# Thresholded attention and a quick-GELU network: scores of the third and fourth pair computed twice, more row sums through DRAM, new ranks

## The chip, the cores and the metric

The kernel runs on one core of a Trainium2 chip. The core has TensorE (matrix products, writing to PSUM), VectorE (DVE in the profile), ScalarE (ACT), GpSimd (POOL) and SyncE (SP, which here only issues DMAs). Each engine executes its own list of instructions strictly in the order in which the program wrote it, and waits on semaphores for the others. The metric is the device time in microseconds of one execution; the times shown are of three runs, and the verdict compares medians.

## The reference

Inputs are q, k, v of shape (8, 8, 576, 64) (batch, heads, sequence, head dimension), a scalar tau, and two float64 weight matrices, 512 x 2048 and 2048 x 512. Cut to what matters:

```python
scores = scale * np.matmul(q, k.transpose(0, 1, 3, 2))
thresh = np.max(scores, axis=-1, keepdims=True) - tau
scores = np.where(scores >= thresh, scores, -1000000000.0)
attn = np.exp(scores - np.max(scores, axis=-1, keepdims=True))
attn = attn / (np.sum(attn, axis=-1, keepdims=True) + 1e-09)
x = np.matmul(attn, v)            # -> (8 * 576, 512), heads side by side
h = x @ w_in
out = (h * (1.0 / (1.0 + np.exp(-1.702 * h)))) @ w_out
```

So each row of scores keeps only what lies within tau of its maximum, and then goes through a softmax. The output of the attention, 4608 tokens of 512, goes through a two-layer network.

## The kernel before

**Pairs.** Two heads of one batch make a pair; there are 32 pairs, n = 0 to 31, four to a batch. Scores stand transposed: keys on the partitions, queries along the free dimension, in nine tiles of 64 keys (j), two of which share an SBUF tile of 128 x 1152 (t = 0 to 3, and a tail of 128 x 576). The steps of a pair are

1. `load_qk`, `load_v`: DMAs from SP; `prep` (L477) transposes q and k on VectorE.
2. `scores` (L493): four 64-row matmuls of 288 columns for each j into PSUM; `keep` (L510) copies the tile to SBUF on ScalarE.
3. `in_groups` with max (L516), `over_tiles` (L525), `over_halves` (L536, L542 or L547): the maximum of each query less tau, on VectorE.
4. These thresholds have to lie along the free dimension on all partitions (the buffer `mb`). For the pairs in `BY_DMA` a small transpose (L553) is followed by two DMAs to a row in DRAM (`row_out`, L566) and two back, spread over the partitions (`row_in`, L575). Pair 2 is not in `BY_DMA`; it uses `spread_max` (L557), a transpose on VectorE.
5. `sub` (L580) subtracts the thresholds on VectorE, `mask` (L586, a steep Prelu) and `exps` (L590) follow on ScalarE.
6. `values` and `sums_by_pe` (both L601, tiles pv and den): products with v, and for pairs 0 to 4 with a matrix of ones. Pairs 5 to 31 sum with `in_groups` (add) on VectorE instead. For pairs 5 to 7 the sums are then spread with `one_group` (L643, L647) and `spread_sums` (L684, L686) on VectorE, from pair 8 on with `turn_sums` (L658 to L663) and DMAs through DRAM (`sums_out`, L668, `sums_in`, L675).
7. `place_x` (L703): divides and writes x, transposed. When the four pairs of a batch are placed, token blocks of 256 can enter the network.

**Weights.** They arrive as float64 in 32 pieces (16 of w_in, then 16 of w_out), by DMAs from POOL (L428, L429), and are turned into float32 by `cv_ex` (L439), `cv_power` (L447, ScalarE), `cv_frac` (L453, L457) and `cv_end` (L465).

**Network.** `mm1_0` (L758), `tanh` and `gelu_0` (L764), `mm2` (L740) do the first two blocks; later blocks use L718, L727, L730 and L909, the last four L823. From pair 7 on the scores of pair n are interleaved with the values of pair n - 2; these stretches are called joints below.

**Order.** The program writes a list of tasks with an engine, an estimated cost, a rank and resources that they take and give back (PSUM slots `psA`, three of them, and `psM`, two; SBUF slots; slots of the DRAM rows). `run_in_order` goes through estimated time and starts on each engine the ready task of lowest rank. Only the order that comes of this is in the program: on the chip, an instruction that waits holds up everything behind it on its engine. The rank of a pair's task is n plus a bias by function, from one table for pairs 0 to 3 (`EARLY`), one for 4 to 7 (`SECOND`) and one for the rest (`LATER`). The weights' tasks have ranks of their own (`W_RANK`, `CV`). Network tasks on TensorE come last in rank and fill what is left, those on the other engines come first.

Of the kernel before, what the change touches and what calls it, by code (L numbers as in the profile page):

```python
# [10 lines left out]
FP32 = mybir.dt.float32  # L11
# [19 lines left out]
def kernel(  # L31
# [84 lines left out]
    stop = const.tile([P, 1], FP32, name="stop")  # L116
    shift = const.tile([P, 1], FP32, name="shift")
# [9 lines left out]
    for x in ("raw0", "raw1", "qkT0", "qkT1", "mb"):  # L127
# [6 lines left out]
        "exps": -11.47,  # L134
        "in_groups": 5.75,
        "keep": 10.66,
        "load_qk": -0.27,
        "load_v": 4.86,
        "mask": -2.66,
        "one_group": -15.86,  # L140
        "one_row": 12.67,
        "over_halves": -7.01,
        "over_tiles": -4.01,
        "place_x": -17.11,
        "prep": -11.73,
        "row_in": 20.49,
        "row_out": 4.47,
        "scores_run": 12.45,
        "spread_max": -1.73,
        "spread_sums": 7.14,  # L150
        "sub": 9.27,
        "sums_by_pe": 0.27,
        "sums_in": -9.39,
        "sums_out": 2.13,
        "turn_rows": -12.55,
        "turn_sums": -0.41,
        "values": 14.64,
        "w_sum": 4.11,
        "x_sum": -14.1,
    }  # L160
    SECOND = {
        "exps": -7.29,
        "in_groups": 20.95,
        "keep": 16.67,
        "load_qk": -8.88,
        "load_v": 5.53,
        "mask": 2.36,
        "one_group": 2.55,
        "one_row": -2.71,
        "over_halves": -12.07,  # L170
        "over_tiles": 2.86,
        "place_x": -20.26,
        "prep": 3.49,
        "row_in": -19.42,
        "row_out": -24.08,
        "scores_run": -7.99,
        "spread_max": -3.11,
        "spread_sums": -2.29,
        "sub": 14.98,
        "sums_by_pe": 35.93,  # L180
        "sums_in": 7.43,
        "sums_out": 4.05,
        "turn_rows": -3.84,
        "turn_sums": 4.03,
        "values": 11.79,
        "w_sum": -10.45,
        "x_sum": -10.98,
    }
    LATER = {
        "exps": 2.01,  # L190
        "in_groups": 10.37,
        "keep": -0.02,
        "load_qk": -6.6,
        "load_v": 3.77,
        "mask": 14.79,
        "one_group": 4.78,
        "one_row": -14.98,
        "over_halves": 1.09,
        "over_tiles": -6.27,
        "place_x": -0.34,  # L200
        "prep": 2.34,
        "row_in": 4.02,
        "row_out": 2.64,
        "scores_run": -11.25,
        "spread_max": -9.44,
        "spread_sums": -6.73,
        "sub": 2.14,
        "sums_by_pe": 1.46,
        "sums_in": 3.78,
        "sums_out": 2.16,  # L210
        "turn_rows": 12.26,
        "turn_sums": 0.29,
        "values": -10.38,
        "w_sum": 6.61,
        "x_sum": 6.02,
    }
    CV = {
        "cv_end": -8.05,
        "cv_ex": 2.22,
        "cv_frac": -11.72,  # L220
        "cv_power": -4.72,
        "load_w": -7.79,
# [4 lines left out]
    QUARTERS = ("scores", "scores_run", "values", "sums_by_pe")  # L227
# [76 lines left out]
    JOINT = 7  # L304

# [183 lines left out]
    def scores(n, j):  # L489
        ps = psA.tile([P, 2, 512], FP32, name="ps", tag="ps")  # L490
        for h in range(2):
            for c in range(2):
                nc.tensor.matmul(  # L493
                    ps[ts(c, KT), h, 0:SH],
                    lhsT=mats[n, 1][ts(h, D), ts(j, KT)], rhs=mats[n, 0][ts(h, D), ts(c, SH)],
                    start=True, stop=True,
                )
        if j == NK - 1:
            del mats[n, 0], mats[n, 1]
        pss[n, j] = ps  # L500
# [31 lines left out]
    def over_halves(n):  # L532
        r = stats[n, ALU.max]
        o = work.tile([P, QB], FP32, name="fold", tag="fold", bufs=1)
        for x in (1, 3) if n in BY_DMA else range(4):
# [3 lines left out]
            )  # L539
        if n in BY_DMA:  # L540
# [10 lines left out]
    def turn_rows(n):  # L551

        nc.vector.transpose(out=flat[1], in_=flat[0])  # L553

# [52 lines left out]
    def values(n, tiles):  # L607
# [4 lines left out]
        if n < NPAIR:  # L612
# [334 lines left out]
    nc.gpsimd.memset(ones, 1.0)  # L947
    nc.gpsimd.dma_start(
# [26 lines left out]
    BY_PE = 5  # L975
    BY_DMA = (0, 1, *range(3, NP))
    SUMS_BY_DMA = range(8, NP)
# [6 lines left out]
    W_RANK = (0, 12.87, 12.51, 22.24, 0, 4.97)  # L984
# [211 lines left out]
    for n in range(NP):  # L1196
# [5 lines left out]
        slow = 1.1 if n < NPAIR else 1.0  # L1202
# [59 lines left out]
        else:  # L1262
            for js in [range(x, x + 3) for x in range(0, NK, 3)] if n >= WHOLE else [[x] for x in range(NK)]:
# [4 lines left out]
                    give=own(n, "qkT0", "qkT1") if js[-1] == NK - 1 else (),  # L1268
# [4 lines left out]
        a = task("DVE", 0.35, r, over_tiles, n, ALU.max, after=mx)  # L1273
        a = task(
            "DVE", 0.8 if n in BY_DMA else 1.05, r, over_halves, n, after=[a, tau_done],
            take=("row",) if n in BY_DMA else (),
        )
        if n in BY_DMA:
            a = task("DVE", 0.21, r, turn_rows, n, after=[a])
            a = task("SP", 0.6, r, row_out, n, after=[a], lag=3.3)  # L1280
# [8 lines left out]
        for t in range(NKT + 1):  # L1289
            tail = t == NKT  # L1290
            a = task(
# [9 lines left out]
        if n < NPAIR:  # L1301

            pv = den = None
            for t in every:
                first = t == 0
                den = task(
                    "PE", (0.97 if t < NKT else 0.484) * slow, r, sums_by_pe, n, [t], True, after=[ws[t], den],
                    take=("psM", "psM") if first else (),
                )
                pv = task(  # L1310
                    "PE", (0.97 if t < NKT else 0.484) * slow, r, values, n, [t], after=[ws[t], den, pv, lv],
                    take=("psA",) if first else (), give=(back[t],) if t < NKT else ("s_t", v_m),
                )
            su = []
            a = task("DVE", 1.07, r, one_row, n, after=[den], give=("psM", "psM"))
        else:
# [3 lines left out]
            if n < BY_PE:  # L1320
                a = task("PE", 4.36, r, sums_by_pe, n, every, False, after=ws + [pv], take=("psA",), give=back)
                a = task("DVE", 1.07, r, one_row, n, after=[a], give=("psA",))
            else:
                su = [
# [51 lines left out]
```

## Time and profile before

| | us |
|---|---|
| median of three runs (lowest, highest) | 1317.49 (1315.77, 1319.47) |
| the profiled execution's own time | 1317.94 |
| its span, first to last instruction | 1316.2 |
| TensorE busy in the span | 1260.9 |
| VectorE busy | 1006.1 |
| ScalarE busy | 646.6 |
| first matmul of the network (L758) starts at | 117.60 |
| last attention write of pair 3 (L703) starts at | 114.40 |

Spans count from the first instruction to the last. Where a table says "idle before" with an arrow, the engine stood still for so long and the arrow names what ended that. Durations of instructions that follow one another directly overlap a little, so a sum over a run of them is made from start to start.

### The profile page before, as it was taken

What the parts mean: (1) busy time and instruction counts of PE and PEld (TensorE: products, weight loads), DVE (VectorE), ACT (ScalarE), POOL (GpSimd) and SP (SyncE); (2) the same over time, 40 slices, a digit from 0 to 9 for tenths busy, and PEclk for the clock granted to TensorE, in tenths of its full rate; (3) what the DMA queues carried; (4) which work ended last, traced back from release to release, by engine and by line L of the source; (5) the groups of instructions that cost most, each with busy time, mean ns of one, the idle gap of its engine ahead of it and who ended that gap; (6) DMA issues with size and microseconds to landing.
All of it is one profiled execution on the core that took longest, in us unless ns stands there. A gap on an engine that the chain in (4) does not pass through costs nothing. (4 is left out here: it accounts for less than half of the span.)

```text
span 1316.2 us, 22807 instructions
## 1 busy us (share of the span) xinstructions
PE 1260.9 (96%) x9128; PEld 975.6 (74%) x9128; DVE 1006.1 (76%) x1610; ACT 646.6 (49%) x830; POOL 249.0 (19%) x291
## 2 busy tenths in 40 slices
PE   5669999999999999999999999999999999999998
PEld 2346864457887777777778888777777778888887
DVE  7989999898888887788777877777888863652642
ACT  4876666576554555555554555454556540210210
POOL 1201211012031211213021303030212117120120
PEclk8879999999999999999999999999999999999999
DMA  8976766545323223212213222323122110000000
GB/s 152 293 189 207 230 207 149 112 77 100 85 55 71 55 55 71 51 50 54 58 42 72 55 71 55 71 55 71 36 55 54 36 46 8 9 1 25 8 0 32
DMA packets 258819, 102.88 MB, mean 78 GB/s; under 512 B 233754, under 2 KB 243994, under 8 KB 258714
## 3 DMA queue, kind: packets, MB, share of 16 engines
q1 hardware_dynamic: 244986, 63.40, 22.4%
q0 software_dynamic: 11360, 37.74, 9.3%
q8 instruction: 71, 1.16, 0.4%
q10 hardware_dynamic: 2368, 0.30, 0.2%
q14 instruction: 34, 0.28, 0.1%
HBM read 87.51 MB, written 9.69 MB: 74 GB/s over the span
## 5 line engine op out<-in xcount | busy, mean ns | idle before, releaser
L516 DVE TRANSPOSE_TENSOR_REDUCE part<-arena 128x36 f32<-128x1152 f32 (+1 forms) x295 | 357.5, 1235 | 41.9 <-ACT arena L510 32.4
L718 PE MATMUL hps<-xT,w_in 128*128 128x256 f32 x1536 | 337.2, 380 | 0.5 <-DVE arena L730 0.4
L718 PEld LDWEIGHTS hps<-xT,w_in 128*128 128x128 f32 x1536 | 290.7, 190 | 45.9 <-issue 5.7
L586 ACT ACTIVATE arena<-arena 128x1152 f32<-128x1152 f32 (+1 forms) x160 | 169.4, 1059 | 144.0 <-DVE arena L580 143.8
L510 ACT COPY arena<-ps 128x576 f32<-128x576 f32 x288 | 170.7, 647 | 115.3 <-PE ps L493 111.9
L580 DVE TENSOR_TENSOR arena<-arena 128x1152 f32<-128x1152 f32 (+1 forms) x158 | 201.1, 1313 | 20.5 <-DMA arena<-row 20.5
L909 PE MATMUL ops<-w_out,arena 128*128 128x256 f32 x896 | 202.4, 380 | 1.8 <-DVE arena L730 1.8
L590 ACT ACTIVATE arena<-arena,shift,scl 128x1152 f32<-128x1152 f32 (+1 forms) x160 | 200.3, 1252 | 4.1
L493 PE MATMUL ps<-arena 64*64 64x288 f32 x2304 | 174.7, 420 | 22.9 <-DVE arena L477 15.3
L909 PEld LDWEIGHTS ops<-w_out,arena 128*128 128x128 f32 x896 | 169.3, 190 | 28.7 <-DVE arena L730 3.1
L875 POOL TENSOR_TENSOR arena<-arena 128x256 f32<-128x256 f32 x56 | 49.7, 888 | 647.1 <-DVE arena L730 543.9
L601 PE MATMUL pv<-arena 64*64 64x288 f32 x2176 | 159.7, 408 | 0.0
L727 ACT ACTIVATE th<-hps 128x512 f32<-128x512 f32 x112 | 66.0, 589 | 186.0 <-PE hps L718 171.8
L909 PE MATMUL ops<-arena 128*128 128x256 f32 x672 | 150.7, 380 | 0.7 <-DVE osb L931 0.7
L493 PEld LDWEIGHTS ps<-arena 64*64 64x64 f32 x2304 | 84.0, 137 | 90.8 <-ACT arena L510 30.4
L909 PEld LDWEIGHTS ops<-arena 128*128 128x128 f32 x672 | 127.1, 190 | 20.4 <-issue 2.2
L601 PEld LDWEIGHTS pv<-arena 64*64 64x64 f32 x2176 | 82.1, 134 | 54.1 <-issue 10.0
L931 DVE SCALAR_TENSOR_TENSOR osb<-ops,osb 128x256 f32<-128x256 f32 x98 | 39.3, 413 | 97.9 <-PE ops L909 90.6
L730 DVE SCALAR_TENSOR_TENSOR arena<-th,hps 128x512 f32<-128x512 f32 x96 | 64.2, 669 | 46.7 <-ACT th L727 46.4
L740 PE MATMUL ops<-w_out,arena 128*128 128x512 f32 x128 | 57.2, 600 | 3.2 <-DVE w_out L465 2.2
L758 PE MATMUL hps<-xT,w_in 128*128 128x256 f32 x256 | 56.4, 381 | 0.0
L888 POOL TENSOR_TENSOR arena<-arena 128x512 f32<-128x512 f32 x28 | 35.6, 1272 | 108.3 <-PE ops L909 108.3
(115 smaller groups left out, 1044.7 us busy)
## 6 DMA issues: line engine op xcount, KB each, us to landing
arena<-in_v_dram SPq DMA_DIRECT2D x128, 144.0 KB
arena<-in_q_dram SPq DMA_DIRECT2D x128, 72.0 KB
out_dram<-osb SPq DMA_DIRECT2D x36, 256.0 KB
arena<-in_k_dram SPq DMA_DIRECT2D x124, 72.0 KB
arena<-row SPq DMA_DIRECT2D x62, 144.0 KB
arena<-row_s SPq DMA_DIRECT2D x48, 144.0 KB
w_out<-in_moe_w_in_dram POOLq DMA_DIRECT2D x12, 512.0 KB, 9.5
arena<-in_moe_w_out_dram POOLq DMA_DIRECT2D x12, 512.0 KB, 6.3
```

Source lines behind the costliest of these rows:

```text
L493: nc.tensor.matmul(ps[ts(c, KT), h, 0:SH], lhsT=mats[n, 1][ts(h, D), ts(j, KT)], rhs=mats[n, 0][ts(h, D), ts(c, SH)], start=True, stop=True,)
L510: nc.scalar.copy(out=sT[n, t][:, u], in_=pss.pop((n, j))[:, :, 0:SH])
L516: nc.vector.tensor_reduce(out=stats[n, op][:, t * 2 * QB : min(2 * t + 2, NK) * QB], in_=sT[n, t].rearrange("p u h (g d) -> p (u h g) d", ...
L580: nc.vector.tensor_tensor(out=s, in0=s, in1=mbs[n].unsqueeze(1).to_broadcast(list(s.shape)), op=ALU.subtract)
L586: nc.scalar.activation(out=s, in_=s, func=AF.Prelu, alpha=STEEP)
L590: nc.scalar.activation(out=s, in_=s, func=AF.Exp, scale=scl, bias=shift)
L601: nc.tensor.matmul(o[c][ts(h, D), 0:SH], lhsT=left(j, h)[ts(c, KT)], rhs=sT[n, t][ts(c, KT), u, h, :], start=(j == 0), stop=(j == NK - 1),)
L718: nc.tensor.matmul(hidden[j][:, ts(f, BLK)], lhsT=w_in[:, c, ds((f * HF + j) * P, P)], rhs=xTs[blk][:, c, :], start=(c == 0), stop=(c == N ...
L727: nc.scalar.activation(out=ths[j], in_=hidden[j], func=AF.Tanh, scale=GELU_SCALE / 2)
L730: nc.vector.scalar_tensor_tensor(out=g[:, :, j, :], in0=two(ths.pop(j)), scalar=1.0, in1=two(hidden.pop(j)), op0=ALU.add, op1=ALU.mult,)
L740: nc.tensor.matmul(acc[i], lhsT=g0[:, j, ts(i, P)], rhs=w_out[:, j, :], start=(j == 0), stop=(j == NFC - 1),)
L909: nc.tensor.matmul(banks[blk][k][:, ts(o, HM)], lhsT=left[:, j, :], rhs=right[:, j, :], start=(j == 0), stop=(j == HF - 1),)
```

## The change

Pairs 2 and 3 (`TWICE`) no longer take their thresholds through `spread_max` or DRAM, and have no `sub` and no `mask`. The scores are computed as before for the maximum. Then `over_halves` writes the thresholds of all four partition quadrants (four L548, four L554), and `row_blocks` makes from them, with a small transpose (L576) and one product with a 0/1 pattern (L578, 128 x 288), a matrix that has each threshold on one partition. `again` (L595) computes the scores of each tile anew, four matmuls, and adds in the same PSUM bank four more with a constant matrix of -1, which subtracts the thresholds. `mask_one` (L603) is the steep Prelu on ScalarE, now reading PSUM, tile by tile of 64 keys; the exponentials follow as before. q and k of the two pairs stay in SBUF until the second computation is done.

Pairs 5, 6 and 7 now spread their sums with `turn_sums`, `sums_out` and `sums_in` through DRAM, as the later pairs did already. All biases, the weights' ranks and some estimated costs and lags in the task list are new, so that the order changes on every engine. Four memsets and four selects on POOL at the start make the two constants. Line numbers of the new kernel are some 12 to 67 higher: L505 is `scores`, L522 `keep`, L528 `in_groups`, L632 `sub`, L638 `mask`, L642 `exps`, L653 values and sums, L755 `place_x`, L810 `mm1_0`, L816 `gelu_0`, L792 `mm2`.

```diff
+    minus = const.tile([P, 2, KT], FP32, name="minus")
+    own_row = const.tile([P, QB // 2], FP32, name="own_row")
...
     EARLY = {
-        "exps": -11.47,
-        "in_groups": 5.75,
+        "again": 6.29,
+        "exps": -15.95,
+        "in_groups": 18.14,
...
+    TWICE = (2, 3)
...
-        if j == NK - 1:
+        if j == NK - 1 and n not in TWICE:
             del mats[n, 0], mats[n, 1]
...
+        if n in TWICE:
+            for x, y in ((0, 0), (1, 2), (2, 1), (3, 3)):
+                nc.vector.scalar_tensor_tensor(
+                    out=flat[0][ts(y, 32), 0:QB], in0=r[ts(x, 32)], scalar=gap[ts(x, 32)],
+                    in1=o[ts(x, 32)], op0=ALU.subtract, op1=ALU.max,
+                )
+            return
...
+    def row_blocks(n):
+
+        nc.vector.transpose(out=flat[1], in_=flat[0])
+        mb = home(n, "mb")[:, 0:SH]
+        nc.vector.tensor_tensor(
+            out=mb.rearrange("p (g i) -> p g i", i=32),
+            in0=flat[1].unsqueeze(1).to_broadcast([P, QB // 2, 32]),
+            in1=own_row.unsqueeze(2).to_broadcast([P, QB // 2, 32]), op=ALU.mult,
+        )
+        mbs[n] = mb
+
+    def again(n, j):
+        ps = psA.tile([P, 2, 512], FP32, name="ps", tag="ps")
+        for first in (True, False):
+            for h in range(2):
+                for c in range(2):
+                    if first:
+                        left = mats[n, 1][ts(h, D), ts(j, KT)]
+                        right = mats[n, 0][ts(h, D), ts(c, SH)]
+                    else:
+                        left, right = minus[ts(h, D), c, :], mbs[n][ts(h, D), :]
+                    nc.tensor.matmul(
+                        ps[ts(c, KT), h, 0:SH], lhsT=left, rhs=right, start=first, stop=not first,
+                    )
...
+    def mask_one(n, j):
+        nc.scalar.activation(
+            out=sT[n, j // 2][:, j % 2], in_=pss.pop((n, j))[:, :, 0:SH], func=AF.Prelu, alpha=STEEP
+        )
...
-    BY_PE = 5
-    BY_DMA = (0, 1, *range(3, NP))
-    SUMS_BY_DMA = range(8, NP)
+    SUMS_BY_PE = (0, 1, 2, 3, 4)
+    BY_DMA = (0, 1, *range(4, NP))
+    SUMS_BY_DMA = range(5, NP)
...
-    W_RANK = (0, 12.87, 12.51, 22.24, 0, 4.97)
+    W_RANK = (23.57, 40.09, 37.91, 6.28, 8.83, 21.44)
...
+            if n in TWICE:
+                for j in range(2 * t, min(2 * t + 2, NK)):
+                    m = task(
+                        "PE", 0.97 * slow, r, again, n, j, after=[m], take=("psA",),
+                        give=own(n, "qkT0", "qkT1", "mb") if j == NK - 1 else (),
+                    )
+                    a = task("ACT", 0.62, r, mask_one, n, j, after=[m] + mx, give=("psA",))
+                ws.append(task("ACT", 0.76 if tail else 1.24, r, exps, n, t, after=[a]))
+                continue
```

## The prediction

> **What bounds the kernel now.** I read the engines' shares first, then TensorE by stretches, then who ends its waits before and after the network begins, then the timeline. From the page's first two parts:
>
> ```profile
> span 1316.2 us, 22807 instructions
> PE 1260.9 (96%) x9128; PEld 975.6 (74%) x9128; DVE 1006.1 (76%) x1610; ACT 646.6 (49%) x830; POOL 249.0 (19%) x291
> ...
> PE   5669999999999999999999999999999999999998
> ...
> DVE  7989999898888887788777877777888863652642
> ```
>
> The table of stretches (span, then busy us of PE, PEld, DVE, ACT):
>
> ```profile
> 117.60:280.00 162.40, 155.98 (x1044) 96.34 (x1041) 153.53 (x252) 101.65 (x128) 20.81 (x34) 0.99 0.61 165
> 280.00:1316.20 1036.20, 1028.37 (x7089) 835.57 (x7087) 750.86 (x1185) 460.02 (x597) 209.45 (x214) 1.00 0.22 50
> ```
>
> From 117.6 us on, where the network's first matmul starts, TensorE works for 155.98 + 1028.37 = 1184.4 of 1198.6 us. Before it works for 76.6. The end is therefore F + 1184.4 + W + 3.4, where F is the start of the network, W TensorE's waits after it, and 3.4 the stretch after the last matmul (ends 1312.8). The waits before and after F:
>
> ```profile
> PE ps L493 <- DVE arena L477: 15.3, 3, 8.3
> PE den L601 <- DVE r L632: 12.9, 2, 10.8
> PE den L601 <- DVE w_out L457: 7.0, 1, 7.0
> ```
>
> ```profile
> PE ps L493 <- ACT arena L510: 4.5, 6, 2.2
> PE ops L740 <- DVE w_out L465: 2.2, 2, 1.6
> PE ops L909 <- DVE arena L730: 1.8, 2, 1.4
> PE ops L740 <- DVE arena L764: 0.9, 1, 0.9
> ```
>
> W is 10.5 with two small ones; 1184.4 + 10.5 + 3.4 is 0.3 short of the 1198.6, so I carry 3.7. Of W, 6.4 lie between 185 and 272 us (0.95, 0.6, 0.91, 1.63, 0.17, 2.16), where VectorE is busy 95% and late: the two waits on ScalarE's copies are copies behind masks that wait for `sub`.
>
> **What the Trainium skill says.** "VectorE: DVE Perf Modes", section on the TRN2 errata, gives (N+151)/0.96 ns for an fp32 tensor_tensor: 1.36 us at 1152, 0.76 at 576; L580 shows 1.31 and 0.75, so it agrees, and prices the new 288-wide product at 0.46. "TensorE: Matmul & The Clock Gate", "What's actually happening", says that an idle window of about 3.4 us halves the clock; here TensorE idles from 70.5 to 81.6 and 74.0 to 86.8 is granted 0.50. "TensorEngine Tiling", "64×64 Mode (4 tiles)", has four independent tiles: four 64-row matmuls take about what one does; here the nine tiles of pair 4's sums, 72 records at two a matmul, take 4.54 us at full clock, so `again`, two such fours, takes 0.97 with its switch of operands. "DMA: Bandwidth & Descriptors", "Anatomy of one DMA", puts a fixed 2 us on a transfer; here pair 0's row leaves at 23.5 and is in use only at 34.67, with the engines full of weights.
>
> **The change on VectorE**, start to start: L580 1.25 and 0.67, L516 1.26, L536 and L542 0.26 each.
> - `sub` of two pairs goes: 8 x 1.25 + 2 x 0.67 = 11.3.
> - Thresholds: pair 2 loses L547 and L557 (0.27 + 0.70) and gets four L554 (1.04), a transpose (0.14) and the product (0.37 to 0.46): +0.6. Pair 3 gets two more L548, two L554 and the product: +1.4.
> - The new order puts four of pair 4's L516 (5.0) and one more piece of weights (2.0) ahead of pair 3's last write.
>
> In sum 99.6 us of VectorE work stand ahead of that write before, and 99.6 - 11.3 + 2.0 + 7.0 = 97.3 after. After the write, the sums of pairs 5 to 7 lose L647, L684 and L686 and keep L658 to L663: 2.55 less 1.39 = 1.16 each. Counted from pair 3's write, the writes of pairs 4 to 7 stand at 47.9, 89.5, 118.1 and 144.1 us of VectorE work, where they stood at 56.7, 96.6, 127.5 and 153.4. TensorE's order needs them earlier too (joints 7 to 10 by 5.3, 3.4, 3.5 and 7.1 us); from joint 11 on it is the same list.
>
> **On TensorE** 18 x 0.97 = 17.5 us are added, all ahead of F; 41.0 us of 117.6 are idle there. Everything ahead of the first L810 (pairs 0 to 3, pair 4's scores, eight tiles of pair 5) and after it is the same work.
>
> **F, step by step.** The start up to 29.3 us is unchanged. Then:
> - VectorE meets pair 0's `sub` at once, but the row is there at 34.6: 5.3 us idle that four L516 (29.33 to 34.67) filled.
> - `sub` of pair 0 to 40.3; pair 1's waits for its row (its packets end at 43.4 in the trace) until 44.5, to 50.2. ScalarE turns pair 0 to 47.3 and pair 1 to 58.5 (2.43 a tile, tail 1.47).
> - TensorE's list has a score tile of pair 3 in the middle of pair 1's sums. Its PSUM slot is freed by a copy that stands on ScalarE behind all of pair 1's exponentials: 59.3. Pair 1's sums are ready at 64.3, where VectorE stands ready at 61.2.
> - With 2.15 for the reciprocals, 3.2 for pair 2's maximum, 0.9 for pair 1's write and 0.5: the matrix for pair 2 is there at 71, pair 3's at 80.
> - Now ScalarE has, in this order, 18 `mask_one` (0.58, as L510 from PSUM), 8 exponentials (1.25) and 2 tails (0.77), among them 8 copies of pair 4 (0.56) and 9 L459 (0.68, as L447): 10.4 + 10.0 + 1.5 + 4.5 + 6.1 = 32.5, from 73. With about 2.5 us of waits for VectorE's L451, pair 3's exponentials end at 108 (101.3 before). TensorE, at 0.97 a tile, is not the limit.
> - Pair 3's sums, pair 2's write, two transposes, one and a half weight pieces and pair 3's write take VectorE to 118; six score tiles of pair 5 follow: F = 120.
>
> So 11.3 us of `sub` leave, and ScalarE's queue becomes what sets F. **W:** of the 6.4 us all go, since VectorE comes 2 to 6 us further ahead of what TensorE needs (8.8 less 5.3 at joint 7, 9.4 less 3.5 at joint 9); the fifth L816 comes 1.3 late (three `sub` and a transpose stand before it): 10.5 - 6.4 + 1.3 = 5.4. The hidden edits: the four L720/L727 DMAs of each sum on SP have 6 us or more of VectorE work before their reader; the constants on POOL end long before 25.9 us, when its first copy runs; without that cover each costs its 2 to 4 us on VectorE only.
>
> Sum: 120 + 1184.4 + 5.4 + 3.7 = 1313.5 us of span, 2.7 below 1316.2. The profiled run's own time is 1317.94, 1.7 above its span; the median is 1.3 above the span, so I expect a median of 1314.8.
>
> **Rivals.**
> - *VectorE's sum sets F after all.* For: it is busy over 90% before F. With the same 15.7 us of idle as before, 97.3 + 15.7 + 2.3 = 115.3 for F, and 1310.1. Against: ScalarE's 32.5 us in one queue. Chance 0.28.
> - *TensorE falls to half clock in front of `again`.* TensorE idles between 55 and 59 and waits again near 70; at half clock a tile costs 1.94, a pair of tiles with its sums 5.8 against ScalarE's 2.4 to 3.6. Pair 2's nine tiles then take 8.7 more, some 7 of it seen: F = 127, the time 1321.8. It decides from F = 126.4, that is once the slow stretch covers most of pair 2. For: 10.8 us of idle did just that at 74. Against: the idle now is 4 us. Chance 0.18.
> - *The later waits stay*, because the new order only moves them: W = 10.5, 1319.9. For: TensorE's joints come earlier by nearly what VectorE gains. Chance 0.12.
> - That the change did not do what it says would show as 158 calls of L632, as L580 has now; the program has 148.
>
> **The numbers.** The first case has 0.42, with a range of its own of 1312 to 1318 (three us of F to either side). Bounds of unknown costs: `mask_one` at 0.55 to 0.66 us moves F by -0.5 to +1.4, the product by 0.2, the row's arrival by 3 us either way. Over 0.3% is 4 us, about what a measurement of this kernel can tell from no change. Faster: 0.26 of the second case and 0.06 of the first. Slower: 0.15 of the third, 0.05 of the fourth, 0.02 of the first. The rest is within. The range 1308.5 to 1322 takes in all four.
>
> **What would show it.** VectorE idle from 29 to 34.6 us; pair 1's `r` (L684) ending TensorE's or VectorE's wait near 64; ScalarE over 90% busy from 73 to 108; L810 from 120 on; of the waits after it those on L477 and L522 nearly gone. I am wrong if F is below 117 or above 125, or if new waits appear after joint 11, where TensorE's list is the same.

## The result, and the profile after

The changed kernel takes 1337.63 us (median of four runs, 1336.28 to 1341.11); the kernel before, now of four runs on the same chip, took 1318.48 (1315.77 to 1322.98). The ratio is 1.0146, 95% interval 1.0111 to 1.0181: slower, by 19 us. The prediction was 1314.8 with a range up to 1322. The profiled execution took 1336.28 us with a span of 1334.5, so it can be set against the predicted span of 1313.5.

The first two parts of the page, as shown for the kernel before:

```profile
span 1334.5 us, 23381 instructions
PE 1281.3 (96%) x9416; PEld 991.3 (74%) x9416; DVE 994.3 (75%) x1600; ACT 641.7 (48%) x838; POOL 251.7 (19%) x301
...
PE   5788899988999999999999999999999999999998
...
DVE  6798899797887787778787877778887863652642
```

TensorE has 20.4 us more to do and VectorE 11.8 less, as the change intends. But of VectorE's first ten digits, 7989999898, six have fallen (6798899797), and only one has risen: it is idle more, ahead of F and just behind it. The table of stretches shows it over equal lengths. First the 212.4 us from F on in the kernel before, then in the changed one, then its whole stretch from F to the end (length; busy PE, PEld, DVE, ACT, POOL; granted clock; DMA share; GB/s):

```profile
117.60:330.00 212.40, 205.21 (x1473) 133.19 (x1470) 198.92 (x319) 134.93 (x172) 33.91 (x48) 0.99 0.61 150
```

```profile
126.26:338.66 212.40, 199.21 (x1328) 130.44 (x1328) 187.22 (x294) 132.88 (x167) 32.63 (x43) 0.97 0.65 155
126.26:1334.50 1208.24, 1187.85 (x8132) 935.49 (x8128) 894.60 (x1419) 555.82 (x724) 229.02 (x246) 0.99 0.28 65
```

VectorE stands idle for 25.2 us there, against 13.5 before, and TensorE for 13.2 against 7.2. By the prediction's formula: F is 126.3 (predicted 120), W is 1208.2 - 1187.9 - 3.7 = 16.7 (predicted 5.4), and TensorE's own work behind F is 1187.9 (1184.4), part of it at a clock of 0.94 between 270 and 350 us. The three differences, 6.3 + 11.3 + 3.5, are the 21 us by which the span missed.

TensorE's waits, first ahead of F, then behind it:

```profile
PE ps L505 <- DVE arena L489: 16.4, 3, 8.1
PE den L653 <- ACT arena L642: 7.2, 5, 4.2
PE den L653 <- DVE r L684: 4.8, 1, 4.8
```

```profile
PE hps L770 <- DVE arena L782: 5.1, 2, 4.8
PE ps L505 <- ACT arena L522: 4.9, 2, 4.3
PE hps L810 <- DVE arena L816: 3.9, 2, 3.1
PE ops L961 <- DVE arena L782: 2.3, 2, 1.9
```

The many small waits between 185 and 272 us are gone, as predicted, but two of 4.3 and 4.8 us have come, at 278 and 314, and one of 3.1 at 156.

The new operations cost what was said (groups by shape: count, busy us and mean ns, idle time before):

```profile
L595 PE MATMUL ps<-arena 64*64 64x288 f32 x144 | 12.3, 404 | 0.0
L595 PE MATMUL ps<-arena,minus 64*64 64x288 f32 x144 | 12.2, 402 | 0.0
L603 ACT ACTIVATE arena<-ps 128x576 f32<-128x576 f32 x18 | 11.2, 637 | 0.6 <-PE ps L595 0.6
L578 DVE TENSOR_TENSOR arena<-flat,own_row 128x288 f32<-128x288 f32 x2 | 0.9, 458 | 0.1
```

What changed ahead of F is seen on POOL, which issues the weights' loads, and on VectorE (start, duration, idle time before it and what ended it; the last line is pair 3's write):

```profile
80.65 0.53 POOL L440 DMA_DIRECT2D w_out<-in_moe_w_in_dram  x1 [42.84 <-ACT arena L642]
```

```profile
94.15 0.43 DVE L465 TENSOR_SCALAR w_out<-w_out 128x512 int32<-128x512 int32 x1 [0.90 <-DMA w_out<-in_moe_w_in_dram]
102.89 0.43 DVE L451 TENSOR_SCALAR arena<-arena 128x512 uint32<-128x512 uint32 x1 [1.10 <-DMA arena<-in_moe_w_in_dram]
105.10 0.43 DVE L465 TENSOR_SCALAR arena<-arena 128x512 int32<-128x512 int32 x1 [1.77 <-DMA arena<-in_moe_w_in_dram]
118.85 0.78 DVE L489 STREAM_TRANSPOSE arena<-arena 128x576 f32<-128x576 f32 x1 [2.41 <-DMA arena<-in_k_dram]
123.05 0.95 DVE L755 TENSOR_TENSOR xT<-pv,arena 128x256 f32<-128x256 f32 x4 [0.19 <-PE pv L653]
```

Weight piece 6 can be loaded only when piece 0 has left its slot, that is behind piece 0's L477. Before, VectorE converted the first pieces at 37 us, under pair 0's `sub`, and POOL went on at 41. Now the new ranks put that conversion at 57.8 to 62 and its last step at 79.4, so six pieces load between 80.7 and 91 and four more from 101.5. The DMA engines, 0.32 busy from 58 to 80 us, are 0.94 busy from 80 to 106, and pair 5's k, which SP issues at 94.6, comes at 118.9. (The label L642 names what ended at that moment on ScalarE; the first experiment shows that it is the L477.)

VectorE did not wait for ScalarE there. ScalarE's last exponential of pair 3 ends at 110.8, and VectorE takes up that pair's sums (L684) at 112.6, straight from other work:

```profile
109.91 0.87 ACT L642 ACTIVATE arena<-arena,shift,scl 128x576 f32<-128x576 f32 x1
```

```profile
108.78 3.89 DVE L528 TRANSPOSE_TENSOR_REDUCE part<-arena 128x36 f32<-128x1152 f32 x3
112.59 0.81 DVE L684 TRANSPOSE_TENSOR_REDUCE r<-den 128x9 f32<-128x288 f32 x2
```

Behind F, VectorE's longest waits for DMAs in the changed kernel:

```profile
154.28 0.78 DVE L489 STREAM_TRANSPOSE arena<-arena 128x576 f32<-128x576 f32 x1 [4.07 <-DMA arena<-in_k_dram]
...
250.76 1.36 DVE L632 TENSOR_TENSOR arena<-arena 128x1152 f32<-128x1152 f32 x1 [2.71 <-DMA arena<-row]
...
257.54 1.08 DVE L755 TENSOR_TENSOR xT<-pv,arena 128x192 f32<-128x192 f32 x4 [2.89 <-DMA arena<-row_s]
...
310.99 2.63 DVE L632 TENSOR_TENSOR arena<-arena 128x1152 f32<-128x1152 f32 x2 [5.77 <-DMA arena<-row]
313.53 0.68 DVE L782 SCALAR_TENSOR_TENSOR arena<-th,hps 128x512 f32<-128x512 f32 x1
```

The first is for pair 6's k, and the L816 that stands behind it is the gelu for which TensorE waits at 156. `row_s` is the row of pair 6's sums, one of the three pairs whose sums now go through DRAM. The L782 behind the late row of pair 9 is the gelu for which TensorE waits 4.85 us at 314.

### The profile page after: what moved, and what is told of

Read it like the earlier page. It is cut to its first block, busy times and chain, and to the rows that moved or that the text cites. A ratio compares the mean times of both kernels' runs of the same rounds, so it can differ in the third digit from the quotient of the medians.

```text
span 1334.5 us, 23381 instructions
## 1 busy us (share of the span) xinstructions
PE 1281.3 (96%) x9416; PEld 991.3 (74%) x9416; DVE 994.3 (75%) x1600; ACT 641.7 (48%) x838; POOL 251.7 (19%) x301
## 5 line engine op out<-in xcount | busy, mean ns | idle before, releaser
L528 DVE TRANSPOSE_TENSOR_REDUCE part<-arena 128x36 f32<-128x1152 f32 (+1 forms) x295 | 357.6, 1236 | 45.8 <-ACT arena L522 33.3
L770 PE MATMUL hps<-xT,w_in 128*128 128x256 f32 x1536 | 339.1, 381 | 5.2 <-DVE arena L782 5.1
L770 PEld LDWEIGHTS hps<-xT,w_in 128*128 128x128 f32 x1536 | 291.6, 191 | 51.6 <-DVE arena L782 6.6
L522 ACT COPY arena<-ps 128x576 f32<-128x576 f32 x288 | 171.3, 645 | 131.6 <-PE ps L505 131.3
L638 ACT ACTIVATE arena<-arena 128x1152 f32<-128x1152 f32 (+1 forms) x150 | 155.1, 1060 | 152.9 <-DVE arena L632 152.1
L632 DVE TENSOR_TENSOR arena<-arena 128x1152 f32<-128x1152 f32 (+1 forms) x149 | 190.8, 1321 | 26.6 <-DMA arena<-row 26.5
L505 PE MATMUL ps<-arena 64*64 64x288 f32 x2304 | 176.0, 422 | 24.8 <-DVE arena L489 16.4
L642 ACT ACTIVATE arena<-arena,shift,scl 128x1152 f32<-128x1152 f32 (+1 forms) x160 | 194.6, 1245 | 1.5
L653 PE MATMUL pv<-arena 64*64 64x288 f32 x2176 | 160.7, 410 | 1.2 <-ACT arena L603 1.2
L505 PEld LDWEIGHTS ps<-arena 64*64 64x64 f32 x2304 | 86.4, 138 | 90.2 <-ACT arena L522 23.1
L653 PEld LDWEIGHTS pv<-arena 64*64 64x64 f32 x2176 | 82.1, 135 | 56.5 <-issue 10.5
L782 DVE SCALAR_TENSOR_TENSOR arena<-th,hps 128x512 f32<-128x512 f32 x96 | 64.3, 671 | 41.6 <-ACT th L779 41.6
L810 PE MATMUL hps<-xT,w_in 128*128 128x256 f32 x256 | 58.5, 389 | 3.9 <-DVE arena L816 3.9
L810 PEld LDWEIGHTS hps<-xT,w_in 128*128 128x128 f32 x256 | 49.3, 194 | 13.2 <-DVE arena L816 4.7
L489 DVE STREAM_TRANSPOSE arena<-arena 128x576 f32<-128x576 f32 x64 | 46.5, 752 | 13.9 <-DMA arena<-in_q_dram 7.0
```

The source lines that it names most:

```text
L505: nc.tensor.matmul(ps[ts(c, KT), h, 0:SH], lhsT=mats[n, 1][ts(h, D), ts(j, KT)], rhs=mats[n, 0][ts(h, D), ts(c, SH)], start=True, stop=True,)
L522: nc.scalar.copy(out=sT[n, t][:, u], in_=pss.pop((n, j))[:, :, 0:SH])
L528: nc.vector.tensor_reduce(out=stats[n, op][:, t * 2 * QB : min(2 * t + 2, NK) * QB], in_=sT[n, t].rearrange("p u h (g d) -> p (u h g) d", ...
L632: nc.vector.tensor_tensor(out=s, in0=s, in1=mbs[n].unsqueeze(1).to_broadcast(list(s.shape)), op=ALU.subtract)
L638: nc.scalar.activation(out=s, in_=s, func=AF.Prelu, alpha=STEEP)
L642: nc.scalar.activation(out=s, in_=s, func=AF.Exp, scale=scl, bias=shift)
```

## The experiments

The theory at this point: A, the ranks made the loads late and let them fall into one heap, which moved F; and the sums' round trips make VectorE wait behind F. The rival B: VectorE's and ScalarE's own lists fill both stretches, and the waits for DMAs lie in gaps that would be there anyway.

Except for the parts undone or done alone (e2, e3, e4, e12), the order is changed by hand: the planner runs as in the kernel that the text names, its list is kept, and single tasks are moved in it:

```diff
-                tasks[i][3](*tasks[i][4])
+                seq.append(i)
...
+        for what, behind in MOVES:
+            i = seq.pop(at(*what))
+            seq.insert(at(*behind) + 1, i)
+        for i in seq:
+            tasks[i][3](*tasks[i][4])
```

The added lines make the line numbers higher, by 27 in e1 and up to 60 in e11; those of e3 are 9 lower, those of e2, e4 and e12 the changed kernel's. All at a glance (ratio to the kernel before on the same chip; F and the span from F to the end from the profiled execution):

| kernel | F | F to the end | ratio (95%) |
|---|---|---|---|
| before | 117.6 | 1198.6 | |
| changed | 126.3 | 1208.2 | 1.0146 (1.0111, 1.0181) |
| e1 weights early | 122.1 | 1204.8 | 1.0086 (1.0055, 1.0118) |
| e2 sums undone | 131.5 | 1201.6 | 1.0116 (1.0085, 1.0146) |
| e3 sums alone | 116.1 | 1212.9 | 1.0100 (1.0064, 1.0136) |
| e4 twice alone | 132.0 | 1214.1 | 1.0181 (1.0143, 1.0219) |
| e5 = e1, sums undone | 125.4 | 1199.6 | 1.0071 (1.0046, 1.0096) |
| e6 = e1, score tile moved | 122.9 | 1205.9 | 1.0088 (1.0069, 1.0107) |
| e7 = e1, mask and row moved | 126.1 | 1204.8 | 1.0109 (1.0090, 1.0128) |
| e8 = e5, waits filled | 122.8 | 1198.3 | 1.0028 (1.0015, 1.0042) |
| e9 = e1, gelus ahead | 125.4 | 1206.3 | 1.0093 (1.0059, 1.0126) |
| e10 = e8, pair 4's k early | 119.3 | 1201.4 | 1.0012 (0.9995, 1.0028) |
| e11 = e10, two pieces later | 116.7 | 1203.6 | 1.0027 (1.0012, 1.0041) |
| e12 ranks alone | 116.2 | 1262.4 | 1.0474 (1.0451, 1.0498) |

F of a single execution scatters. Up to F the changed kernel and e2 have the same order of instructions on every engine, and F is 126.3 and 131.5; e1, e5, e7 and e9 have another order in common, and F is 122.1, 125.4, 126.1 and 125.4. So a difference of some 4 us in F between two rows shows nothing by itself; it has to be read together with the waits, and with the medians.

**e1: weights early.**

```diff
+        (('cv_ex', 0), ('in_groups', 2, 0)),
+        (('cv_frac', 0), ('cv_ex', 0)),
...
+        (('cv_power', 0), ('exps', 0, 4)),
...
+        (('cv_end', 0), ('sub', 1, 4)),
...
+        (('load_w', 6), ('cv_end', 2)),
...
```

Pieces 1 and 2 follow piece 0 at each of these places, and the loads of pieces 7 and 8 that of piece 6.

> The changed kernel in its own order, with one thing moved: VectorE converts weight pieces 0 to 2 while it waits for pair 1's row (39.8 to 45.1 us), instead of at 57.8 and 79.4, so that the loads of pieces 6 to 8 go out near 53 instead of 80.6, when the DMA engines have little to do. TensorE's order is the same. Theory A (the loads of the weights come in one heap between 80 and 105 us, and VectorE's waits for them, 0.90 + 1.10 + 1.77, and for pair 5's k, 2.41, are what moved F from the predicted 120 to 126.3): these waits shrink to under 2 us in all, F falls to 120 to 122, the time to 1331 to 1333. Theory B (VectorE's own work and ScalarE's queue fill that stretch, and the waits for DMAs only lie in gaps that would be there anyway): F stays at 125 to 127 and the time within 1.5 us of the changed kernel's 1337. Both: ScalarE's three L459 ahead of pair 1 cost up to 1 us on pair 1's sums.

Measured 1330.35 us, F 122.1. POOL's load of piece 6 goes out at 51.5:

```profile
51.46 0.53 POOL L467 DMA_DIRECT2D w_out<-in_moe_w_in_dram  x1 [14.27 <-DVE w_in L504]
```

VectorE's waits for weights are 0.34 and 1.82, and its wait for pair 5's k is gone. This is not one lucky execution: from 80 us to pair 3's write VectorE waits 6.2 and 10.3 us for weights and k in the two kernels with late loads (changed, e2), and 1.3 to 2.9 in the five with early ones (e1, e5, e6, e7, e9). F is 124.8 on average in the four that share e1's order, 128.9 in the two that share the changed kernel's. The conversions also fill VectorE's wait for pair 1's row (5.31 in the changed kernel, 0.82 in e1), but that is not the gain: it comes back in front of pair 1's `one_row` (1.46 in the changed kernel, 6.01 in e1), which starts at 65.4 instead of 63.6. So about 4 us of F and 7 us of the median were the late loads. A holds, with the time a little below its range.

**e2: sums undone.**

```diff
-    SUMS_BY_DMA = range(5, NP)
+    SUMS_BY_DMA = range(8, NP)
```

> The changed kernel with the sums of pairs 5 to 7 spread by VectorE again, as before the change; thresholds twice and the new ranks stay, TensorE's order is nearly the same. Theory A (the two round trips of the sums and the rows share SP's queue, so pair 9's row goes out late and VectorE waits 5.8 us for it near 305, and the waits of TensorE at 278 and 314, 9.2 us in all, come from there): the wait at 314 goes, W falls from 16.6 to 8 to 12, time 1329 to 1333, F unchanged at 126. Theory B (VectorE's order after F is what is late, and the sums through DRAM save it 3.5 us): W stays at 15 to 20, the time 1337 to 1341.

Measured 1334.54. From F to the end it takes 6.6 us less than the changed kernel, and the wait at 314 is 1.75 and 0.59 instead of 4.85, as A said; but W, 13.8, and the time lie between the two theories, and F is not the same, 131.5 against 126.3, with the same order ahead of F. VectorE waits for the same k:

```profile
123.12 0.78 DVE L489 STREAM_TRANSPOSE arena<-arena 128x576 f32<-128x576 f32 x1 [6.91 <-DMA arena<-in_k_dram]
```

6.91 us instead of 2.41: with the DMA engines 0.85 and 0.94 busy from 80 to 106 us, the wait for this k differs by 4.5 us between two executions of one order, and F with it. The gain of 3 us in the medians is less than the 6.6 behind F.

**e3: sums alone**, on the kernel before (the same edit the other way round).

> The kernel before, with one part of the change alone: the sums of pairs 5 to 7 by rows through DRAM, old ranks and old planner's costs. F unchanged at 117.6. Theory A (sums through DRAM collide with the rows on SP): W rises from 10.5 to 14 to 18, time 1321 to 1326. Theory B (they save VectorE 1.16 us a pair and are hidden): W 7 to 10.5, time 1314 to 1318.

Measured 1331.26: 13.7 us slower by this part alone, more than A said. F is hardly changed (116.1), from F to the end it takes 14.3 more. TensorE's and VectorE's lines at the two places:

```profile
250.88 0.95 DVE L746 TENSOR_TENSOR xT<-pv,arena 128x192 f32<-128x192 f32 x4 [3.45 <-DMA arena<-row_s]
...
311.92 0.78 DVE L480 STREAM_TRANSPOSE arena<-arena 128x576 f32<-128x576 f32 x1 [10.20 <-DMA arena<-in_q_dram]
```

```profile
269.24 2.20 PE L496 MATMUL ps<-arena 64*64 64x288 f32 x16 [7.54 <-ACT arena L513]
...
314.51 5.91 PE L761 MATMUL hps<-xT,w_in 128*128 128x256 f32 x13 [7.24 <-DVE arena L773]
```

The first DVE line is the write of pair 6, which waits for its sums: they leave at 243.7 and are in use at 250.9. The write stands ahead of the next pair's work in the order, so everything behind it waits too, up to the mask in front of the copy that TensorE needs at 269. At 302 VectorE stands in front of pair 11's q, which SP could issue only at 301.3, behind the rows, while the second of POOL's two copies of 1 MB is under way; behind it stands the gelu.

**e4: twice alone.**

```diff
-    SUMS_BY_DMA = range(5, NP)
+    SUMS_BY_DMA = range(8, NP)
...
-    W_RANK = (23.57, 40.09, 37.91, 6.28, 8.83, 21.44)
+    W_RANK = (0, 12.87, 12.51, 22.24, 0, 4.97)
```

This is the changed kernel with all but the scores set back; the tables of biases and the costs are the old ones too, except for the three new functions.

> The kernel before, with one part of the change alone: the scores of pairs 2 and 3 twice on TensorE, with the old ranks and weights (the three new functions have the changed kernel's ranks). In this order VectorE has 111.6 us of work and 19 weight pieces ahead of pair 3's last write, where it had 99.6 and 12 before, so that the first loads are early but more conversion stands ahead of F. Theory A (only the late weights spoil the change; scores twice are worth what the prediction gave them): 1312 to 1318. Theory B (what VectorE's list holds ahead of pair 3's write sets F, weights included: 111.6 plus 12 to 16 us of waits): F 126 to 130, with up to 7 pieces fewer to do after it, time 1320 to 1330.

Measured 1343.98, F 132.0; B was nearer, and the size was beyond both. VectorE has 19 pieces ahead of pair 3's write and waits 4.29 and 3.10 us for a pair's q and k (at 90.7 and 97.1). Behind F one wait stands out:

```profile
260.94 2.20 PE L505 MATMUL ps<-arena 64*64 64x288 f32 x16 [11.68 <-ACT arena L522]
```

So early loads alone are not enough: the old ranks, with tasks they were not made for, give an order that is worse than the new one.

**e5: early weights, sums undone** (both edits above).

> The kernel of the experiment with early weights (pieces 0 to 2 converted in the wait for pair 1's row), and the sums of pairs 5 to 7 spread by VectorE again. Theory A (early weights and sums each cost on their own: the weights in F, the sums in what TensorE loses after F): F 121 to 123 as with early weights, what TensorE loses after F 12 to 14 us against 16.7, time 1325 to 1328. Theory B (one waits for the other, so that the second gain is given back): 1329 to 1332.

Measured 1326.92; from F to the end 1199.6, which is the kernel before's 1198.6 again. Against e1 the sums cost 5.1 us behind F, against the changed kernel's 6.6 (e2) and the 14.3 of e3. The stretch of 212.4 us from F on, e1 first, then e5:

```profile
122.12:334.52 212.40, 200.57 (x1384) 130.49 (x1384) 189.49 (x301) 135.72 (x172) 34.43 (x46) 0.98 0.63 154
```

```profile
125.36:337.76 212.40, 205.23 (x1468) 133.08 (x1466) 198.18 (x315) 140.72 (x178) 35.55 (x44) 0.99 0.61 150
```

With the sums through DRAM VectorE is idle for 22.9 us, without for 14.2. They save VectorE 3.5 us of work by the prediction's count (1.16 a pair), and it stands idle 8.7 us longer. The time is A's; F is above A's 121 to 123, in the scatter of that order, and W, 11.5, just below A's.

Of the 19 us the two parts explain about half. In ratios, early weights are worth 0.60% (changed to e1) and 0.45% (e2 to e5), that is 6 to 8 us. The sums undone are worth 0.30% (changed to e2) and 0.15% (e1 to e5), 2 to 4 us, which in the times alone is hardly clear of noise. Behind F it is: with the sums through DRAM (changed, e1, e6, e7, e9) it takes 1204.8 to 1208.2 us from F to the end, without (e2, e5, e8, e10, e11) 1198.3 to 1203.6. With both, 0.71% or 9 us remain.

**e6: tile behind.**

```diff
+        (('scores_run', 3, [0]), ('sums_by_pe', 1, [4])),
+        (('keep', 3, 0), ('scores_run', 3, [0])),
```

> The kernel of the experiment with early weights, with one thing moved on TensorE: pair 3's first score tile stands behind pair 1's last tile of sums instead of in the middle of them. Its PSUM slot comes free only behind pair 1's exponentials on ScalarE. Theory A (VectorE's work sets F from 60 us on, and its 6 us of idle time ahead of pair 1's one_row are lost time): pair 1's one_row starts at 60 to 62 instead of 65.4, F 118 to 119.5, time 1326 to 1328. Theory B (ScalarE's queue from 73 us on sets F, as the prediction had it): one_row comes earlier, but F stays at 121 to 123, time 1329 to 1331.

Measured 1330.42, F 122.9, in B's ranges and not to be told from e1, but for another reason than B's. Pair 1's `one_row` starts at 65.5 though pair 0's row came 2.6 us later than in e1 (`sub` at 35.23, 32.60 in e1), so the tile gave about what the row took; VectorE still waits 4.4 us for pair 1's sums. Those had waited for something else as well: in e1 TensorE's first sum of pair 1 stands 6.5 us for the L684 of pair 0's `one_row` (there L711), which frees its PSUM slots and stands behind pair 1's `sub`.

**e7: two moves behind F.**

```diff
+        (('mask', 8, 0), ('keep', 9, 3)),
+        (('sums_in', 8), ('row_in', 9)),
```

> The kernel of the experiment with early weights, with two things moved behind F, each at one of TensorE's two long waits. On ScalarE pair 8's first mask goes behind two more copies of pair 9's scores (at the wait of 4.34 us near 272); on SP the sums' row of pair 8 is read back behind pair 9's row instead of ahead of it (at the wait of 4.35 us near 307). Theory A (a copy that stands behind a mask waiting for sub, and a row that stands in SP's queue behind the wait for the sums' own landing, are what TensorE waits for): the first wait falls under 1 us, the second to 1 to 2.5 us, time 1324 to 1327. Theory B (VectorE is late at both places, and the full DMA engines at the second; the moves only shift the wait by a tile): 1328 to 1331.

Measured 1332.5, and from F to the end the same 1204.8 as e1. TensorE's lines at the two places:

```profile
278.62 2.20 PE L534 MATMUL ps<-arena 64*64 64x288 f32 x16 [3.67 <-ACT arena L551]
309.96 10.63 PE L799 MATMUL hps<-xT,w_in 128*128 128x256 f32 x48 [3.06 <-DVE arena L811]
323.13 10.63 PE L799 MATMUL hps<-xT,w_in 128*128 128x256 f32 x48 [2.54 <-DVE arena L811]
```

The first wait moved by a tile (4.34 to 3.67), the second came back in two parts (4.35 to 3.06 and 2.54). B holds, though the time is a little above its range: the place in a queue was not it.

**e9: gelus ahead**, the other attempt at the second wait.

```diff
+        (('place_x', 8), ('in_groups', 10, 3)),
+        (('in_groups', 10, 4), ('keep', 10, 8)),
+        (('gelu', 0), ('t_minus', 3, 0)),
+        (('sub', 9, 0), ('gelu', 0)),
+        (('sub', 9, 1), ('sub', 9, 0)),
+        (('gelu', 1), ('sub', 9, 3)),
+        (('sub', 9, 2), ('gelu', 1)),
+        (('sub', 9, 3), ('sub', 9, 2)),
```

> The kernel of the experiment with early weights (all sums of pairs 5 to 7 through DRAM), with VectorE's order changed near 300 us alone: the first two L782 of the second block, pair 8's last write and one L528 stand ahead of pair 9's sub, which waits 5.26 us for its row. Theory A (TensorE's wait of 4.35 us near 307 is a gelu that stands behind a sub whose row is late): it falls under 1.5 us, the time to 1326 to 1328 with F at 122, what TensorE loses after F from 16.7 to 13 to 14 us. Theory B (VectorE is behind TensorE there with or without the row): the wait comes back within 10 us at the next gelu or the next joint, 1329 to 1331.

Measured 1332.22. The wait of 4.35 is now three, of 4.5 in all:

```profile
310.96 3.72 PE L805 MATMUL hps<-xT,w_in 128*128 128x256 f32 x16 [1.48 <-DVE arena L817]
316.50 3.72 PE L805 MATMUL hps<-xT,w_in 128*128 128x256 f32 x16 [1.82 <-DVE arena L817]
321.43 10.63 PE L805 MATMUL hps<-xT,w_in 128*128 128x256 f32 x48 [1.21 <-DVE arena L817]
```

B again, with the time a little above its range. By these two, VectorE is what TensorE waits for in this stretch, whichever instruction stands in front. What did shorten the wait, in e5, was time that VectorE didn't lose.

**e8: waits filled**, **e10** and **e11**, from e5 on: can an order be found in which the scores twice pay?

```diff
+        (('in_groups', 2, 0), ('turn_rows', 1)),
...
+        (('sub', 1, 2), ('one_row', 0)),
...
+        (('cv_ex', 5), ('in_groups', 2, 3)),
...
+        (('cv_end', 5), ('row_blocks', 2)),
...
+        (('load_qk', 4, 0), ('row_in', 1)),
+        (('load_qk', 4, 1), ('load_qk', 4, 0)),
...
+        (('cv_ex', 12), ('place_x', 3)),
...
```

The first four of these, with their like for the other tiles and pieces (three L528 ahead of pair 0's `sub`, three `sub` of pair 1 behind pair 0's `one_row`, pieces 5, 3 and 4), and the moves of e1 and e6 make e8. The two loads are added in e10, pieces 12 and 15 in e11.

> The changed kernel with the sums of pairs 5 to 7 spread by VectorE, and with its order ahead of F changed by hand so that VectorE's waits for the rows hold work: three of pair 2's L528 stand ahead of pair 0's sub, pieces 0 to 2 are converted in the wait for pair 1's row, pair 0's one_row stands between pair 1's sub (pair 1's sums wait for its PSUM slots), pair 3's first score tile stands behind pair 1's sums, and pieces 3 to 5 are converted in the 6 us ahead of pair 1's one_row. No piece of weights and no other work is moved past F. Theory A (VectorE's list plus its waits set F, the 9 to 12 us of waits from 30 to 65 are what the change added, and scores twice are otherwise as cheap as the prediction had them): F 113 to 117, what TensorE loses after F 11 to 13 us, time 1313 to 1318, which is as fast as the kernel before or a little faster. Theory B (ScalarE's queue from the thresholds of pair 2 on sets F): F 118 to 121, time 1319 to 1323.

e8 measured 1322.83, F 122.8: the time is B's, F above B's. The waits from 30 to 65 us fell from 10.0 in e1 to 3.4 (0.90 and 2.52), but the gain came back as two others:

```profile
87.82 0.78 DVE L540 STREAM_TRANSPOSE arena<-arena 128x576 f32<-128x576 f32 x1 [4.96 <-DMA arena<-in_k_dram]
...
116.89 0.43 DVE L516 TENSOR_SCALAR w_out<-w_out 128x512 int32<-128x512 int32 x1 [2.08 <-DMA w_out<-in_moe_w_in_dram]
```

Pair 4's k was now the one that shared the DMA engines with weights; neither wait is for ScalarE.

> The kernel of the filled order (sums of pairs 5 to 7 on VectorE), with one thing moved on SP: the loads of pair 4's q and k go out ahead of the loads of v for pairs 2 and 3, near 47 us instead of 70 to 82, where k shared the DMA engines with weight pieces 9 to 11 and VectorE stood 4.96 us in front of its transpose. Theory A (this wait is what gave back the gain of the filled waits): it goes, F 117 to 119.5 instead of 122.8, time 1317 to 1320. Theory B (ScalarE's queue, which was full from 72 to 106 us, sets F by itself): F 121 to 123, time 1321 to 1323.

e10 measured 1319.97, F 119.3: the wait is gone and F 3.5 us earlier, as A said. The ratio, 1.0012 (0.9995 to 1.0028), can't be told from 1. Of the 9 us that e5 kept, the filled waits of e8 took back some 6 and these loads about 2.

> The kernel with pair 4's loads early, and in addition weight pieces 12 and 15 are converted behind pair 3's last write instead of ahead of it (they are first read some 40 us after F), so that VectorE does 3.6 us less ahead of that write and doesn't wait 2.1 us for their loads. Theory A (VectorE's list ahead of pair 3's write sets F): F 3 to 5 us below that of the kernel with pair 4's loads early, 113 to 116; behind F the two pieces delay the first gelus and cost 0 to 2 us; time 1314 to 1317, a little below the kernel before. Theory B (TensorE's last scores or ScalarE set F): F within 1 us of the other, time the same or 1 to 2 us longer.

e11 measured 1322.49. F falls to 116.7, by 2.6 us, a little less than A said; pair 3's write then waits 2.56 us for TensorE's product with v. But from F to the end the profiled execution takes 2.2 us more than that of e10. In the first 30 us behind F TensorE waits 0.58, 1.29 and 0.93 us for VectorE's first gelus (L876), where e10 has one wait of 0.27: VectorE's work moved past F is not hidden there. The median is 2.5 us higher than e10's, with overlapping intervals; that the move gains nothing is shown, that it costs is not.

**e12: ranks alone**, on the kernel before.

```diff
-    TWICE = (2, 3)
-    BY_DMA = (0, 1, *range(4, NP))
-    SUMS_BY_DMA = range(5, NP)
+    TWICE = ()
+    BY_DMA = (0, 1, *range(3, NP))
+    SUMS_BY_DMA = range(8, NP)
```

> The kernel before with the new ranks, the new weights' ranks and the new planner's costs alone; scores of pairs 2 and 3 and the sums of pairs 5 to 7 are worked out as before the change. VectorE again converts pieces 0 to 2 only after pair 1, so that the loads of pieces 6 to 8 wait for them. Ahead of pair 3's last write the list has 92.6 us of work with 8 weight pieces, where the kernel before has 99.6 with 12. Theory A (the ranks carry the late weights, whatever the scores do): the loads of pieces 6 to 8 go out after 65 us, F 117 to 124, and with fewer pieces ready at F TensorE loses 16 us or more after F; time 1324 to 1336. Theory B (the ranks are harmless by themselves, and the cost is in the scores twice and the sums): 1316 to 1321.

Measured 1380.38, 63 us slower, far beyond both. The loads are as late as A said, and the weights of the second product are what TensorE then waits for:

```profile
83.98 0.53 POOL L440 DMA_DIRECT2D w_out<-in_moe_w_in_dram  x1 [45.65 <-DVE w_in L477]
```

```profile
241.90 2.08 PE L792 MATMUL ops<-w_out,arena 128*128 128x512 f32 x2 [9.79 <-DVE w_out L477]
262.23 5.52 PE L792 MATMUL ops<-w_out,arena 128*128 128x512 f32 x8 [14.16 <-DVE w_out L477]
```

The three parts alone cost 13.7, 26.4 and 63.3 us, all at once 19: they don't add. That each set of ranks fits one set of tasks is the likely reading; no run here separates the ranks from the costs and lags set with them.

## Why the prediction was wrong, step by step

- **The new operations: right.** `again` took 0.97 us a tile and TensorE's added work is 20.4 us in all, of which 17.5 are these. The rival with half clock fell: from 58 to 105 us the granted clock was 1.00. L578 took 0.46, L603 0.64 (0.58 assumed, within its bounds).
- **The walk up to 80 us: right, with some luck.** VectorE's wait for row 0 was 2.8 (5.3 said); pair 1's `sub` began at 45.1 (44.5); pair 1's `one_row` at 63.6 (64.3); the matrices at 70.1 and 79.0 (71 and 80). In six other kernels with the same order up to there the row's `sub` began anywhere from 29.9 to 36.7.
- **VectorE's work: right.** Start to start and without its idle time, it has 98.4 us of work ahead of pair 3's write, 1.9 less than before (2.3 said). From there to the writes of pairs 4 to 7 the work is 8.9, 7.0, 9.1 and 8.9 us less than before (8.8, 7.1, 9.4 and 9.3 said). What failed is what this was taken to mean for the time.
- **"ScalarE's queue becomes what sets F": wrong.** Its exponentials ended at 110.8 (108 said). The waits for L451 were 1.36, 1.10 and 1.99 instead of 2.5 in all, and two of the three L451 or the L465 ahead of it waited for a weight's DMA. TensorE's last sums of pair 3 ended at 111.5, and VectorE came to them at 112.6, without a wait. So the path to F was VectorE's work and waits: 98.4 + 24.6 is 123.0, pair 3's write, and F follows 3.2 later; before it was 100.3 + 14.1 and 3.2. That is the path of the first rival, which went wrong in the idle time alone (15.7 said). e10 and e11, where F fell with VectorE's waits and work, bear it out.
- **"Pair 3's sums, pair 2's write, ... and pair 3's write take VectorE to 118; F = 120": the step that failed for F.** It counts VectorE's work and no load. The four waits for loads shown above are 6.2 us, and F missed by 6.3. The list of POOL, with its load 42.8 us behind the one before, was there to be read from the order, but the step moved the conversions ("one more piece of weights", 2.0 us) without asking what their slots release. e1 takes 4 us of these waits away. The Trainium skill says in "DMA: Bandwidth & Descriptors", section "Issuing engines are not separate DMA queues", that transfers of all issuers interleave on the same 16 engines; this trace agrees: SP's four DMAs for pair 5's k took 10.18 us to issue among POOL's weights, those for pair 4's 3.12 at 71.9.
- **"W: of the 6.4 us all go, since VectorE comes 2 to 6 us further ahead": the step that failed for W.** The small waits went, and others of some 12 us came. The step took VectorE's work for its time. Counted from pair 3's write, the writes of pairs 4 to 7 came only 2.9, 1.1, 0.1 and 0.8 us earlier than before, for all the work saved; against what TensorE's order needs (5.3, 3.4, 3.5 and 7.1) VectorE is 2 to 6 us further behind. It is idle for 25.2 us of the first 212 instead of 13.5. (In the stretch from 185 to 272 us before, which the prediction calls 95% busy, it was busy for 80.3 of 87 us, 92%.)
- **"The four L720/L727 DMAs of each sum on SP have 6 us or more of VectorE work before their reader; ... each costs its 2 to 4 us on VectorE only": one part of that idle time.** Pair 6's sums needed 7.2 us in e3 and 6.2 in the changed kernel from SP's first issue to the reader, with only 3.7 and 3.3 us of work to cover it; VectorE waited 3.45 and 2.89. The size was right, "on VectorE only" was not: undoing this part takes 5.1 to 6.6 us off the stretch behind F, and doing it alone adds 14.3.
- **The 6.4 us were not gained without the sums either.** With the sums as before, W is 13.8, 11.5, 10.8 and 12.9 (e2, e5, e8, e10), where it was 10.5 before. In e5 the writes come 6.7, 4.5, 4.4 and 5.3 us earlier, which leaves VectorE within 2 us of where it was against TensorE's needs. Which waits hold the rest of its time was not tested.
- **The rival that ended slower named the wrong mechanism**; that its F of 127 is close to 126.3 is chance. The range of 1308.5 to 1322 left no room for two unknowns, the DMA engines' load ahead of F and SP's trips behind it, that both turned out badly.
- The bounds given for being wrong were half met: F is above 125. The new waits lie ahead of joint 11, not behind it.

What stays open: whether scores twice gain anything in an order made for them. In e10 they cost nothing that can be told (the sums as before); e11 shows that work taken out of the way of F delays the first gelus behind it. No kernel here was faster than the one before.

## What to carry to other kernels

When an order changes, follow the slots as well as the work: a conversion that moves 20 us moves the next load by the time until its slot is freed, and the load then lands among others. An operation taken off a busy engine in exchange for a DMA round trip saves its duration and costs the engine's wait for the trip; read from the trace how long such trips take at that hour, not how long one takes alone. And an estimate of an engine's lead from its work alone holds only while its idle time stays as it was: here the work came out to half a microsecond, and the lead was lost in waits.

## What was not expected of the hardware

- In seven kernels with the same order up to that point, pair 0's `sub` found its row at 32.7 (changed), 30.0 or earlier (e2), 32.6 (e1), 29.9 or earlier (e5), 35.2 (e6), 36.7 (e7) and 35.7 us (e9), with the DMA engines 0.74 to 0.79 busy from 24 to 36 us; and the same k of pair 5 made VectorE wait 2.41 us in one kernel and 6.91 in another. So the arrival of one small load among large ones varied by 4 to 7 us. In the kernel before, four L528 (there L516) covered the row's spread.
- One of POOL's copies of 1 MB within the core takes 9.8 to 11.0 us from issue to landing (changed, e3). A row that SP sent out in the stretch of these copies was in use 9.8 us later (changed: 301.2 to 311.0), and pair 11's q took 10.6 (e3: 301.3 to 311.9).
